# An attention-and-experts kernel on one core: attention re-ordered by unit with the k side ahead, the kv copy on ACT's own DMA queue, routing in pieces, and expert slots by rank with eight early slots

## The chip, the cores and the metric

One core of a Trainium2 chip. The metric is the device time of one execution in microseconds. Times are medians of executions; the span is the time from the first to the last instruction in one profiled execution, 1.6 to 1.9 us shorter than the time of that execution. (The profiled execution of the kernel before took 435.7 us, 4.5 below its median, so its stages are some 1% short.) All ratios compare executions of state "fast" only. Engines are named as the profile names them: PE (matmul), PEld (its weight loads), DVE, ACT, POOL, SP. Inputs are the same draw in every run.

## The reference, cut to what matters

```python
# q, k, v: 8 batches x 8 heads x 576 positions x 64
q_p, k_p = phi(q), phi(k)              # relu, times cos and sin of the position: 128 features
kv  = einsum('bhsf,bhsd->bhfd', k_p, v)
num = einsum('bhsf,bhfd->bhsd', q_p, kv)
den = einsum('bhsf,bhf->bhs', q_p, k_p.sum(2)) + 1e-6
x   = (num / den) as 4608 tokens of 512
e_idx = argmax(x @ w_gate)             # 8 experts, one per token
out   = gate * sigmoid(x @ w_output_gate)[e_idx] * (relu(x @ w1[e]) @ w2[e])
```

Attention is done in four groups of two batches. Its rows are scattered by expert into a buffer in DRAM (`xs`), and the experts then run 43 *slots* of 128 rows of one expert each. A table in SBUF says for each slot which expert it is and where its rows begin. Because the expert is known only at run time, the engines load table entries into registers.

## The kernel before

The slot loop. PE works through x transposes of the next slot, h transposes of the last one, first layer (`hp`, 8 matmuls), second layer of the last slot (`yp`, 8 matmuls). Two register loads stand between the transposes and the first layer.

```python
def layer1(j):
    ev = PE.value_load(evs[0:1, j:j + 1], min_val=0, max_val=7)      # which expert
    wv = PE.value_load(wns[0:1, j:j + 1], min_val=32, max_val=256)   # weights that must be in
    PE.wait_ge(wsem, wv)
    ...
    for fh in range(2):
        ...                                   # 4 matmuls on wt[:, ev, ...], then relu on ACT

for j in range(NSLOT + 1):
    if j + 4 < NSLOT: fetch(j + 4)            # SP: 128 rows of xs, at a row from the table
    if j + 1 < NSLOT: x_tr(j + 1)             # PE transposes, DVE copies xts
    if j >= 1:        hts = h_tr(j - 1)       # PE transposes, DVE copies hts
    if j < NSLOT:     layer1(j)
    if j >= 1:        layer2(j - 1, hts)      # PE, then DVE scales y, POOL scatters it
    ...
```

All routing is finished, and the table made in one block on DVE, before slot 0. In attention, heads are paired so that each query matmul finds its kv in its own half of the partitions; there is no copy of kv. v is loaded by 64 DMAs with rows of 256 B.

Of the kernel before, what the change touches and what calls it, by code (L numbers as in the profile page):

```python
# [21 lines left out]
def kernel(  # L22
# [12 lines left out]
    PE = nc.tensor  # L35
# [15 lines left out]
    NSLOT = 43  # L51
    XW = DM + 4
# [60 lines left out]
    for qd in range(4):  # L113
        hA = 4 * (qd // 2) + qd % 2
        for ab in range(2):
            h = hA + 2 * ab
            DVE.tensor_copy(wpr[0:64, qd, 32 * ab:32 * ab + 16], wg0[0:64, h, :])
            DVE.tensor_copy(wpr[64:128, qd, 32 * ab + 16:32 * ab + 32],
                            wg0[64:128, h, :])
# [16 lines left out]
    jv_i = constp.tile([P, NSLOT], I32, name="jv_i")  # L136
    GP.iota(jv_i[:], pattern=[[1, NSLOT]], base=0, channel_multiplier=0)
    jv = constp.tile([P, NSLOT], F32, name="jv")
# [8 lines left out]
                      iota8[:].unsqueeze(1).to_broadcast([P, E, E]), ALU.is_ge)  # L147

# [9 lines left out]

    EW = 4 * F + 8 * DM
# [3 lines left out]
    wsem = tc.alloc_semaphore("wsem")  # L163

    def load_w(e):
        for d in (GP.dma_start(w1v[:, e], moe_w1[e].rearrange("(c p) f -> p c f", p=128)),
                  GP.dma_start(w2v[:, e],
                               moe_w2[e].rearrange("(c p) d2 -> p c d2", p=128))):
            d.then_inc(wsem, 16)
            tc.add_to_no_dep_group("w", d.ins)  # L170

    def own(e, lo):
        return wt[:, e, lo:lo + 4096].bitcast(F32)

    kbuf = [own(7, 4096 * i).rearrange("p (h c d) -> p h c d", h=H, d=D) for i in range(2)]
    qbuf = [own(6, 4096 * i).rearrange("p (h c d) -> p h c d", h=H, d=D) for i in range(2)]
    KW = H * NC4 * 65 * 2
    v0 = wt[:, 4:6, :].rearrange("p e w -> p (e w)")
    vbuf = [v0[:, KW * i:KW * i + KW].bitcast(F32).rearrange(
        "p (h c d) -> p h c d", h=H, d=65) for i in range(2)]  # L180
    for i in range(2):
        GP.memset(vbuf[i][:, :, :, 64:65], 1.0)
# [3 lines left out]
    evs = constp.tile([P, NSLOT], I32, name="evs")  # L186
    wns = constp.tile([P, NSLOT], I32, name="wns")
    rows_i = constp.tile([P, NSLOT], I32, name="rows_i")
    valid = constp.tile([P, NSLOT], U8, name="valid")
    sidx = constp.tile([P, NSLOT], I32, name="sidx")  # L190
    GP.memset(sidx[:], BIG)

    with tc.tile_pool(name="wk", bufs=2) as wk, \
         tc.tile_pool(name="pqo", bufs=2, space=bass.MemoryType.PSUM) as pqo, \
         tc.tile_pool(name="pkv", bufs=1, space=bass.MemoryType.PSUM) as pkv, \
         tc.tile_pool(name="ptr", bufs=2, space=bass.MemoryType.PSUM) as ptr:



        zt = wk.tile([P, XW], U16, name="zt", tag="xr", bufs=14)  # L200
# [3 lines left out]
        tails, kvps, kvms, kcs, qrs, qTs, us = {}, {}, {}, {}, {}, {}, {}  # L204
        ktcs = {}

        def halves(dst, src, b, w=D):
            for hf in range(2):
                SP.dma_start(dst[:, 4 * hf:4 * hf + 4, :, 0:D],
# [6 lines left out]
        def load_v(b):  # L216
            for h in range(H):
                SP.dma_start(vbuf[b % 2][:, h, :, 0:D],  # L218
                             v[b, h, 0:512, :].rearrange("(p c) d -> p c d", c=NC4))
# [22 lines left out]
        def k_prep(b, c):  # L242

            if c == 4 and b % 2 == 1:
                return
            nm = "kc" if c < 4 else "ktc"
            kc = wk.tile([P, 2, H, D], F32, name=f"{nm}{b}_{c}", tag=nm,
                         bufs=2 if c < 4 else 1)
            src = kbuf[b % 2][:, :, c, :] if c < 4 else tails[b // 2, "k"][:]
            ACT.activation(kc[:, 0], src, AF.Relu, scale=cosc[:, c:c + 1])  # L250
            DVE.tensor_scalar(kc[:, 1], src, sinc[:, c:c + 1], 0.0, ALU.mult, ALU.max)  # L251
            if c < 4:
                kcs[b, c] = kc
            else:
                ktcs[b // 2] = kc

        def k_mm(b, c):
# [4 lines left out]
            kc = kcs.pop((b, c)) if c < 4 else ktcs[b // 2]  # L262
            p0, p1 = (0, P) if c < 4 else (lo, lo + 64)
            for hf in range(2):
                for pr in range(2):
                    for cs in range(2):
                        for ab in range(2):
                            h = 4 * hf + pr + 2 * ab
                            rhs = (vbuf[b % 2][:, h, c, :] if c < 4
                                   else vtl[p0:p1, h, :])  # L270
                            o = 130 * pr + 65 * cs
                            PE.matmul(kvp[64 * ab:64 * ab + 64, hf, o:o + 65],  # L272
                                      kc[p0:p1, cs, h, :], rhs,
                                      start=(c == 0 and pr == 0 and cs == 0),
                                      stop=(c == 4), skip_group_check=True)


        def g_evac(b):
            kvp = kvps[b]
            kvm = wk.tile([P, 8, 81], F32, name=f"kvm{b}", tag="kvm", bufs=3)  # L280
            kvms[b] = kvm
            DVE.tensor_copy(kvm[:, 0:4, 0:65],
                            kvp[:, 0, 0:260].rearrange("p (a w) -> p a w", w=65))
            ACT.copy(kvm[:, 4:8, 0:65],
                     kvp[:, 1, 0:260].rearrange("p (a w) -> p a w", w=65))
            kvc = wk.tile([P, 8, 64], F32, name=f"kvc{b}", tag="kvc", bufs=1)
            DVE.tensor_copy(kvc[:], kvm[:, :, 0:64])
# [181 lines left out]
        for i, (b, c) in enumerate(units):  # L469
            g = b // 2  # L470
            if c == 0:

                if b + 1 < B:
                    load_q(b + 1)
# [224 lines left out]
```

## Time and profile before

Median 440.2 us in the runs beside the changed kernel. Stages of the profiled execution (span 433.8 us), read from the PE timeline; the prediction shows the busy times:

| stage | us |
|---|---|
| start to first query matmul | 38.4 |
| group 0 / 1 / 2 / 3 of attention | 37.5 / 39.8 / 56.7 / 34.4 |
| last attention matmul to first expert matmul ("handover") | 37.3 |
| experts, first to last matmul | 182.0 |
| tail | 7.7 |

(The prediction puts the border between groups 2 and 3 at 170.8, inside the last unit of group 2; the first query matmul of group 3 starts at 172.4, and the tables here use that.)

One slot on PE's timeline (start, duration, engine, line, output and inputs, count; a bracket would give idle time before it):

```profile
301.00 1.89 PE L635 MATMUL yp<-wt,hts 128*128 x8
302.73 0.39 PE L595 MATMUL xtsp<-ident,xg 128*128 128x128 f16 x4
302.95 0.61 PE L607 MATMUL htsp<-ident,hs 128*128 128x128 f16 x8
303.40 1.89 PE L623 MATMUL hp<-wt,xts 128*128 x8
```

There is no bracket (gaps under 0.15 us get none): from `hp` at 299.28 to `hp` at 303.40 the array does not wait, 4.12 us per slot.

### The profile page before, as it was taken

The numbers are of one execution on the slowest core, as the hardware profiler recorded it, in microseconds if no ns is written. First come the engines' busy times: TensorE is split into PE (matmuls) and PEld (weight loads), VectorE is DVE, ScalarE is ACT, GpSimd is POOL, SyncE is SP. The second block draws the span as 40 slices with busy tenths as digits, with TensorE's granted clock in tenths as the row PEclk, the third lists the DMA queues.
The fourth block names the chain that finished last, engine by engine and source line by source line (L and its number), as shares of the span: only waits on it lengthen the run. The fifth ranks groups of instructions, "written<-read, shape, count | busy, mean of one in ns | idle before, by whom it ended". The sixth has DMA issues, their size and how long they took to land.

```text
span 433.8 us, 10053 instructions
## 1 busy us (share of the span) xinstructions
PE 319.4 (74%) x3468; PEld 214.5 (49%) x3468; DVE 205.7 (47%) x616; ACT 160.4 (37%) x291; POOL 142.8 (33%) x192
## 2 busy tenths in 40 slices
PE   0706897988885647974100499999999999999991
PEld 0605786766674536753000255555555555555550
DVE  6102576886767125775560234344443443434431
ACT  1304587675756235664100132322323323223230
POOL 2000232338635444248476024221222222212221
PEclk9965999999899577999555699999999999999998
DMA  7999694897899986804916999992323223233100
GB/s 160 243 206 300 175 225 134 223 249 225 196 218 203 327 206 133 131 16 88 202 61 131 225 217 188 222 239 88 110 74 103 94 78 111 63 101 110 62 25 0
DMA packets 90719, 66.88 MB, mean 154 GB/s; under 512 B 51886, under 2 KB 83118, under 8 KB 90672
## 3 DMA queue, kind: packets, MB, share of 16 engines
q1 hardware_dynamic: 72960, 35.26, 33.2%
q0 software_dynamic: 17712, 30.98, 31.4%
q8 instruction: 31, 0.51, 0.5%
q14 instruction: 16, 0.13, 0.1%
HBM read 67.61 MB, written 17.22 MB: 196 GB/s over the span
## 4 chain that ended last, share of the span: by engine, by line
issue 31%; DMA 18%; PE 17%; POOL 13%; DVE 8%; SPq 7%; ACT 3%; POOLq 1%; another core or an unknown queue 0%; DVEq 0%; ACTq 0%
DMA xs<-xr,di 12%; POOL out_dram L643 9%; PE qo L340 6%; PE kvp L272 6%; SPq L218 4%; DMA wt<-in_v_dram 4%; PE qtp L322 3%; POOL xs L428 3%; DVE u L352 2%; DMA wt<-in_q_dram 2%; DMA vtl<-in_v_dram 1%; ACT t L351 1%; SPq L447 1%; DVE kc L251 1%; PE kvtp L294 1%
## 5 line engine op out<-in xcount | busy, mean ns | idle before, releaser
L628 ACT ACTIVATE hs<-hp 128x512 f16<-128x512 f32 x86 | 51.3, 597 | 155.9 <-PE hp L623 155.9
L643 POOL DMA_INDIRECT out_dram<-ysb,sidx x43 | 42.6, 991 | 143.8 <-DVE ysb L641 140.8
L623 PE MATMUL hp<-wt,xts 128*128 x344 | 82.5, 383 | 2.4 <-DVE sidx L600 1.2
L635 PE MATMUL yp<-wt,hts 128*128 x344 | 81.3, 379 | 1.1 <-DVE hts L609 1.1
L360 POOL TENSOR_TENSOR xr<-u,rc 128x512 f16<-128x512 f32 x36 | 40.9, 1137 | 121.6 <-DVE rc L359 121.5
L641 DVE TENSOR_SCALAR ysb<-yp,xg 128x512 f32<-128x512 f32 x43 | 32.3, 750 | 102.4 <-PE yp L635 102.4
L272 PE MATMUL kvp<-wt,kc 128*64 128x65 f32 x1024 | 41.4, 240 | 22.5 <-ACT kc L250 13.8
L352 DVE SCALAR_TENSOR_TENSOR u<-qo,sinc,t 128x324 f32<-128x324 f32 x72 | 37.4, 552 | 40.8 <-ACT t L351 32.4
L340 PE MATMUL qo<-kvm,qT 64*128 64x162 f32 x512 | 48.3, 331 | 8.7 <-ACT qT L324 2.7
L635 PEld LDWEIGHTS <-hts 128*128 128x128 f16 x344 | 33.7, 98 | 41.5 <-DVE hts L609 1.2
L272 PEld LDWEIGHTS kvp<-wt,kc 128*64 128x64 f32 x1024 | 36.9, 152 | 27.9 <-issue 14.6
L623 PEld LDWEIGHTS <-xts 128*128 128x128 f16 x344 | 32.6, 99 | 34.2 <-issue 3.0
L351 ACT ACTIVATE t<-qo,cosc 128x324 f32<-128x324 f32 x72 | 36.9, 529 | 30.7 <-PE qo L340 25.1
L340 PEld LDWEIGHTS qo<-kvm,qT 64*128 64x128 f32 x512 | 40.3, 203 | 12.9 <-ACT qT L324 6.2
L428 POOL DMA_INDIRECT xs<-xr,di x36 | 35.8, 995 | 10.0 <-POOL xr L427 9.8
L595 PE MATMUL xtsp<-ident,xg 128*128 128x128 f16 x172 | 17.1, 223 | 27.6 <-DMA xg<-xs 27.6
L322 PE MATMUL qtp<-ident,qr 128*128 128x128 f32 x144 | 25.4, 303 | 13.1 <-ACT qr L315 13.1
L595 PEld LDWEIGHTS <-xg 128*128 128x128 f16 x172 | 13.3, 99 | 37.6 <-DMA xg<-xs 27.9
L609 DVE COPY hts<-htsp 128x1024 f16<-128x1024 f16 x43 | 29.2, 680 | 0.3 <-PE htsp L607 0.3
L598 DVE COPY xts<-xtsp 128x512 f16<-128x512 f16 x43 | 17.8, 414 | 20.7 <-PE xtsp L595 19.7
L607 PE MATMUL htsp<-ident,hs 128*128 128x128 f16 x344 | 26.4, 219 | 0.2 <-ACT hs L628 0.2
L322 PEld LDWEIGHTS qtp<-ident,qr 128*128 128x128 f32 x144 | 16.3, 149 | 20.0 <-ACT qr L315 14.9
(131 smaller groups left out, 293.7 us busy)
## 6 DMA issues: line engine op xcount, KB each, us to landing
wt<-in_moe_w_dram POOLq DMA_DIRECT2D x16, 1024.0 KB, 14.6
wt<-in_k_dram SPq DMA_DIRECT2D x16, 512.0 KB, 6.2
wt<-in_v_dram SPq DMA_DIRECT2D x64, 128.0 KB, 5.5
wt<-in_q_dram SPq DMA_DIRECT2D x16, 512.0 KB, 6.0
xg<-xs SPq DMA_DIRECT2D x43, 129.0 KB, 2.4
xs<-zt SPq DMA_DIRECT2D x9, 129.0 KB, 4.7
kt<-in_k_dram SPq DMA_DIRECT2D x8, 128.0 KB, 3.8
vtl<-in_v_dram SPq DMA_DIRECT2D x8, 128.0 KB, 4.6
```

The lines of the kernel that those rows point to most:

```text
L272: PE.matmul(kvp[64 * ab:64 * ab + 64, hf, o:o + 65], kc[p0:p1, cs, h, :], rhs, start=(c == 0 and pr == 0 and cs == 0), stop=(c == 4), skip ...
L322: PE.transpose(tp[:, i, :], qrf[:, 128 * i:128 * i + 128], ident[:])
L340: PE.matmul(qo[:, 2 * ab + pr, 0:162], lhs, kvms[b][r0:r0 + 64, 2 * qd:2 * qd + 2, :], start=True, stop=True)
L351: ACT.activation(t[:], qo[:, :, 0:81], AF.Copy, scale=cosc[:, c:c + 1])
L352: DVE.scalar_tensor_tensor(u[:, 4 * hf:4 * hf + 4, :], qo[:, :, 81:162], sinc[:, c:c + 1], t[:], ALU.mult, ALU.add)
L360: GP.tensor_tensor(xrow[:, 0:DM].bitcast(F16).rearrange("p (h d) -> p h d", d=D), u[:, :, 0:64], rc[:].unsqueeze(2).to_broadcast([P, H, D] ...
L428: d = GP.indirect_dma_start(out=xs[:, :], out_offset=bass.IndirectOffsetOnAxis(ap=di[:, c:c + 1], axis=0), in_=xr[:], in_offset=None)
L623: mm = PE.matmul(hp[:], xts[:, kc, :], wt[:, bass.ds(ev, 1), kc * F + fh * 512:kc * F + fh * 512 + 512], start=(kc == 0), stop=(kc == 3))
L628: ACT.activation(hs[:, fh * 512:(fh + 1) * 512], hp[:], AF.Relu)
L635: mm = PE.matmul(yp[:], hts[:, fc, :], wt[:, bass.ds(ev, 1), 4 * F + fc * DM:4 * F + fc * DM + DM], start=(fc == 0), stop=(fc == 7))
L641: DVE.tensor_scalar(ysb[:], yp[:], xg[:, DM + 2:DM + 4].bitcast(F32), None, ALU.mult)
L643: d = GP.indirect_dma_start(out=out[:, :], out_offset=bass.IndirectOffsetOnAxis(ap=sidx[:, j:j + 1], axis=0), in_=ysb[:], in_offset=None, ...
```

## The change

Its intent: start PE sooner (v in large rows, k side up to three units ahead), take routing out of long blocks, and fill the hole at the handover by letting the first eight slots run on tiles of experts that are already full after three groups, with weights loaded in order of that rank. A new query layout makes kv needed in both partition halves, hence a copy. The core of a long diff:

```diff
         def load_v(b):
-            for h in range(H):
-                SP.dma_start(vbuf[b % 2][:, h, :, 0:D],
-                             v[b, h, 0:512, :].rearrange("(p c) d -> p c d", c=NC4))
+            halves(vbuf[b % 2], v, b)                 # two DMAs, rows of 1 KB
 ...  # k_prep: a copy of v into rows of 65 on ACT
+                ACT.copy(vc[:, :, 0:D], vbuf[b % 2][:, :, c, :])
 ...  # the kv copy
+        def g_dup(b):
+            kvd = kvds[b]
+            ACT.dma_start(kvd[0:64, 8:16, :], kvd[64:128, 0:8, :])
+            ACT.dma_start(kvd[64:128, 8:16, :], kvd[0:64, 0:8, :])
 ...  # routing and tables are generators, one step() per unit or three per slot
+            if j == 0:
+                pending.append(late_table())          # slots 8 to 42
 ...  # slots
-            ev = PE.value_load(evs[0:1, j:j + 1], min_val=0, max_val=7)
-            wv = PE.value_load(wns[0:1, j:j + 1], min_val=32, max_val=256)
-            PE.wait_ge(wsem, wv)
+            PE.wait_ge(wsem[0], wa)      # wa, wb: loaded one slot ahead
+            PE.wait_ge(wsem[1], wb)
+        def regs(j):
+            evr[j] = [PE.value_load(tcol(m, j), min_val=lo, max_val=hi)
+                      for m, lo, hi in ((0, 0, 7), (1, 16, 112), (3, 16, 144))]
 ...  # the loop
+            if j >= 1 and j + 1 < NSLOT:
                 x_tr(j + 1)
             if j >= 1:
                 hts = h_tr(j - 1)
             if j < NSLOT:
                 layer1(j)
             if j >= 1:
                 layer2(j - 1, hts)
+            if j + 1 < NSLOT:
+                regs(j + 1)
+            for _ in range(3):
+                step()
```

Two semaphores now count the weights, so PE loads three numbers per slot (rank, two thresholds) and loads them one slot ahead, after the second layer.

## The prediction

> **What bounds the kernel now.** I read the page's second part (40 slices) first, for stages.
>
> ```profile
> PE   0706897988885647974100499999999999999991
> PEclk9965999999899577999555699999999999999998
> DMA  7999694897899986804916999992323223233100
> ```
>
> One slice is 10.8 us. From slice 23 on (experts) PE is full at full clock and DMA is at a third; before it PE is 60 to 90% busy, with a hole at slices 2-3, a dip at 12-14 while DMA is full, and four almost empty slices, 18 to 22. The timeline gives the borders: first query matmul at 38.4 us, groups of two batches (nine units each) start at 75.9, 115.7 and 170.8, the last attention matmul ends at 206.8, the first expert matmul starts at 244.1, the last ends at 426.1. Over these stretches I asked for the busy times (columns: stretch, us, then PE, PEld, DVE, ACT, POOL with counts, granted clock, DMA share, GB/s):
>
> ```profile
> 75.90:115.70 39.80, 32.63 (x566) 27.57 (x567) 30.20 (x90) 27.25 (x52) 22.92 (x29) 0.96 0.83 224
> 115.70:170.80 55.10, 36.85 (x558) 31.66 (x562) 26.54 (x86) 24.90 (x47) 23.00 (x30) 0.78 0.99 218
> 170.80:206.80 36.00, 25.41 (x398) 20.64 (x391) 26.49 (x82) 22.15 (x44) 19.83 (x26) 0.99 0.49 91
> 206.80:244.10 37.30, 1.79 (x21) 1.31 (x20) 13.27 (x55) 1.01 (x3) 19.08 (x28) 0.50 0.69 144
> 260.00:426.10 166.10, 165.01 (x1111) 89.31 (x1109) 71.07 (x156) 46.98 (x79) 42.38 (x44) 1.00 0.40 110
> ```
>
> Group 1 is bound by PE with little slack (32.6 of 39.8). Group 2 has the same work but takes 15 us more, at DMA 0.99. Handover: 37 us without PE. Experts: PE all the time. The waits and the chain say who ended the holes:
>
> ```profile
> PE xtsp L595 <- DMA xg<-xs: 27.6, 2, 26.7
> PE qtp L322 <- ACT qr L315: 13.1, 1, 13.1
> PE kvp L272 <- DMA wt<-in_v_dram: 8.7, 3, 4.9
> DVE u L352 <- POOL xr L360: 8.3, 4, 4.1
> 130.09 15.67 DMA wt<-in_v_dram
> ```
>
> The first is the handover: fetches wait for the slot table, made after the last routing, and for its scatters on POOL. The second is the start: the first q load lands at 35.15 us, behind 16 small v loads and nine zero stores. The third and fifth: in group 2 v loads land late, beside two weight loads. The fourth: at the end of group 3, POOL's scatters hold up the row products, these the u buffers.
>
> [...]
>
> ```profile
> DMA packets 90719, 66.88 MB, mean 154 GB/s; under 512 B 51886, under 2 KB 83118, under 8 KB 90672
> ```
>
> 64 v loads x 512 rows of 256 B are 32,768 of the 51,886, because v lands in rows of 65. While v goes with k (12 to 16 us) the trace moves 179-201 GB/s; at 34 to 36, mostly q and k, 361. [...] the trace has 0.50 at 206.8-244.1, and the first eight expert matmuls take 3.19 us against 1.89 later. So a hole costs another one to two microseconds after it.
>
> **The change part by part.**
>
> *Start.* v comes in two DMAs per batch instead of eight (1 KB rows), q before k of batch 1, and zero stores move to unit 5. SP pays about 0.63 us per issue, so 14 v issues fewer are 9 us and the nine stores 4.5 us. k, v, tails, q of batch 0 are 3.7 MB, some 15 us. ACT then sets the k side: per chunk a v copy into 65-wide rows (estimate 0.63, as qr's 0.626 for equal shape) and relu 0.725, from v's landing at about 12: five chunks end at 18, matmuls at 19.3. Then evacuation 1.3, kvtp 0.65, kvT 0.6, query transpose, kvgp 0.66, copy 0.3: 23.5; and new, the half-swap of kv by two ACT DMAs, 1.2 to issue and about 2.5 to land: 27.5. Against 38.4: -11.
>
> *A unit.* PE's work stays: qo 1.30, qtp 0.59, kvp 1.12 per chunk, kvtp 0.6, kvgp 0.6, routing 0.73. A group of nine with two batches of k side is 11.7 + 5.3 + 11.2 + 2.5 + 0.7 = 31.5. ACT loses the 36 relu passes of qr (22.5 us; relu goes into the transposes' evacuation) and gains 32 v copies (20 us): a group is qT 5.3, t 9.5, v 5.0, k 6.5, evacuations 1.9, exps 0.5, DMA issue 2.4 = 31. DVE: u 9.9, output for two chunks at a time 7.1 (was 10), k 4.9, kv 2.3, routing 5.2 = 29. So three engines stand at 29 to 31.5; none has much slack, and both qo buffers now belong to one unit, released by ACT and DVE only after all eight matmuls. Gained is the wait between evacuation and kvtp, now a unit apart (2.5 us per batch before, at 51.8 and 68.7), and the routing in threes instead of a block (85 to 94 in the chain). I take 36 for groups 1 and 2 (before 39.8 and 55.1): -4 and -19, the latter because both weight loads leave group 2, and v's packets shrink to a quarter. Demand then is 3.5 MB per batch, 18 us, 195 GB/s, under the 224 of group 1.
>
> *Groups 0 and 3.* "Three units ahead" moves k work forward: group 0 does 13 chunks and not 10, 35 us of PE, and batch 1's copy sits at the end of unit 3 with its first use in unit 4, 6 us of chain in the open. 43, against 37.5: +5.5. Group 3 keeps two chunks, 21 us of PE; the loop qo, t, u, next qo (1.3 + 0.06 + 0.55 + 0.6, or t, t, qT 1.7) and DVE at 3.3 per unit bound it: 30.5 against 36, -5.5.
>
> *Handover.* The first eight slots come from tiles already full after three groups. I worked out the router from the reference: counts then are 305, 416, 565, 0, 674, 568, 114, 814; the rank by two groups is expert 4, 2, 7, 1, 6, 5, 0, 3; full tiles 5 and 4, so slots 0-4 are expert 4 and 5-7 expert 2: the table always fills. What remains after the last matmul: DVE u, output, last early piece, about 4 us; but POOL has in the last three units four row products (1.14 each) and nine scatters (0.97 + gap; the copy at each is gone, so about 1.1): 14.5 us in 6.6, so the last scatter of group 2 issues 4.6 after the end; it lands 3.8 later (median of the issues), fetch 2.4 plus issue 0.6, transposes, copy and the second slot 1.6: 13. Against 37.3: -24.
>
> *Experts.* Same matmuls, 43 slots at 4.12 = 177, before 182. The remaining routing and late table, some 45 DVE operations of 0.2 to 0.5, fall into the first four slots: 6 to 7 us of DVE in slots 1 and 2 against 4.12, some 4 us slip; the weight wait at 249 (1.2) goes. 184: +2. Weights: rank 2 is issued at slot 4 and used from slot 13, 37 us for 14.6-23 us loads; the others have more. Tail 7.7, unchanged.
>
> Sum: 27.5 + 43 + 36 + 36 + 30.5 + 13 + 184 + 7.7 = 377.7 of span, against 433.8. Measured times lay 1.9 (profiled) to 6.4 us above it. I predict 379.
>
> **The rivals.** (a) ACT takes the bound: [...] has v copies and DMA issues (each waiting on DVE) between evacuations. For it: 31 against PE's 31.5. Then groups 0 to 2 take 41-46 each, about 395. Against it: before ran group 1 with DVE at 30.2 in 39.8 despite stalls. (b) The pipeline works as meant: PE over 95% in groups 1-2 (33), no stall at unit 4, group 3 at 27: about 364. For it: between 56.9 and 67 PE has gaps of 0.2 us only. (c) The early slots don't help: POOL's queue (weight load of rank 1 waits for rank 0[...]) shifts the wait to the fetch or to slot 5. Rank 1 is issued about 3 us after the attention and has some 30 until slot 5; if it came at 35 or POOL lagged 10 us more, 390. (d) DMA still bounds groups 0-2: if 220 GB/s were the cap whatever the packets, group 0's 12 MB would take 55, giving 390.
>
> **Range and chances.** All single failures leave it under 400, so faster is nearly sure: 0.98, within 2% 0.01, slower 0.01. (a) and (c) together give the high end, (b) the low: 363 to 396.
>
> **What would show it.** First qo at 25-30 us; groups 1-2 at 34-38 us each with PE above 85%, ACT above 80%, DMA below 0.85; no v wait over 2 us; PE idle 10-16 us at the handover, ended by a fetch behind a scatter on POOL; packets under 512 B down to about 19,000; expert stretch 181-187. It is wrong if groups 1-2 are over 40, if the hole moves to slot 5 or 8, or if expert slots rise above 4.2 us after the eighth.

## The result

The changed kernel took 457.5 us (median of four runs, 456.2 to 463.2, the longest slow) against 440.2 in the same rounds: ratio 1.038, 95% interval 1.032 to 1.044, so slower. Ratios here and below are the mean time of one kernel's fast runs over that of the other's fast runs of the same rounds, and so not quite the quotient of the medians quoted.

That was not the whole result. The same text was run twice more: 441.7 us, ratio 1.003 (0.996 to 1.010), and 458.8 us, ratio 1.036 (1.030 to 1.042). The kernel before stood at 440 to 442 each time. So about 62 us of the error against 379 are there every time, and 16 more come and go with the occasion.

| stage (us of span) | before | predicted | changed, 1st set | changed, 2nd set |
|---|---|---|---|---|
| start | 38.4 | 27.5 | 27.2 | 27.3 |
| group 0 | 37.5 | 43 | 57.0 | 57.0 |
| group 1 | 39.8 | 36 | 45.4 | 38.5 |
| group 2 | 56.7 | 36 | 42.4 | 35.3 |
| group 3 | 34.4 | 30.5 | 35.0 | 34.7 |
| handover | 37.3 | 13 | 16.5 | 18.3 |
| experts | 182.0 | 184 | 226.3 | 222.8 |
| tail | 7.7 | 7.7 | 6.9 | 6.9 |

The first expert matmul really does come 21 to 33 us sooner than before (223.4 and 211.1 against 244.1). The experts lose 41 to 44. The slices of the first set (tenths of busy time in 40 equal stretches of 11.4 us):

```profile
PE   0529749798789968681455897889888899899883
PEclk9965859899889987955597899999999999999998
```

From the 26th slice to the last but one PE is at 8 and 9 at full clock, where before it was a row of 9s. That is the slots. The stages of the first set (stretch, us, then PE, PEld, DVE, ACT and POOL busy with counts, granted clock, DMA share, GB/s):

```profile
27.20:84.20 57.00, 40.99 (x653) 35.05 (x653) 21.99 (x53) 28.82 (x55) 9.19 (x8) 0.73 0.74 216
84.20:129.50 45.30, 37.88 (x568) 30.57 (x566) 25.52 (x75) 25.76 (x52) 16.77 (x17) 0.89 0.68 199
129.50:171.90 42.40, 35.91 (x572) 29.03 (x567) 26.29 (x73) 24.97 (x50) 20.29 (x20) 0.94 0.52 154
206.90:223.40 16.50, 1.35 (x18) 1.27 (x19) 10.07 (x33) 1.31 (x4) 7.34 (x8) 0.50 0.73 147
260.00:449.70 189.70, 165.29 (x1076) 82.91 (x1076) 72.46 (x150) 38.88 (x38) 49.41 (x51) 1.00 0.61 136
```

PE is the fullest engine in these groups, but only 72, 84 and 85% of the time, so it is waits that lengthen attention; beside them the granted clock of group 0 was 0.73 (0.50 in two stretches, 26.9 to 43.9 and 54.2 to 67.8 us). In the last line PE is busy 165 of 190 us; the kernel before, from the same moment to the end of its experts, was busy 165 of 166 for about the same matmuls. The waits name who ended them (engine, output, line, what it waited for: us in total, times, longest):

```profile
PE xtsp L631 <- PE yps L682: 17.8, 33, 0.8
PE qo L378 <- DMA wt<-wt: 17.3, 5, 6.5
PE yps L682 <- DVE hts L649: 11.4, 3, 6.1
PE qo L383 <- issue: 7.0, 13, 1.0
```

Each of these four lines led to an experiment. The third is explained under "The late table"; the fourth is what comes and goes. All four are from the first set; the second set has the first three too (17.5, 18.1 and 7.2 us) and not the fourth.

*The slot.* PE's timeline late in the changed kernel:

```profile
406.14 1.89 PE L682 MATMUL yps<-wt,hts 128*128 x8
408.52 0.39 PE L631 MATMUL xtsp<-ident,xg 128*128 128x128 f16 x4 [0.49 <-PE yps L682]
408.75 0.61 PE L646 MATMUL htsp<-ident,hs 128*128 128x128 f16 x8
409.19 1.89 PE L667 MATMUL hp<-wt,xts 128*128 x8
```

`hp` to `hp` is now 4.78 us. "Waits for PE yps" sounds like a dependency between matmuls, but nothing in the transposes needs `yps`; the bracket only says that `yps` was what ended last before them. The sequencer's own records show what lies between: 

```profile
L653 PEldq TENSOR_LOAD <-tab x111: 295/302/948, 263.0 to 441.5; - x111
```

Three loads per slot, here at 406.48, 407.16 and 407.84, so 0.68 us apart: 0.30 for the load itself, 0.15 for a register operation, 0.02 for a bounds test, the rest between these records. The last is done at 408.46 and the transposes begin at 408.51.

*The first wait for the kv copy.*

```profile
27.23 0.88 PE L378 MATMUL qo<-wt,qT 64*128 64x162 f32 x2 [0.49 <-DVE wt L341]
34.37 2.52 PE L378 MATMUL qo<-wt,qT 64*128 64x162 f32 x14 [6.26 <-DMA wt<-wt]
```

The first matmuls come at 27.23, the predicted 27.5, but they are those that don't need the copy. The rest of the unit waits 6.26 us for it, and runs at a granted clock of 0.50 after, as it was in the wait (2.52 us for 14 instead of some 1.3).

### The profile page after: what moved, and what is told of

It reads as the page before. It is cut to its first block, busy times and chain, and to the rows that moved or that the text cites. A ratio compares the mean times of both kernels' runs of the same rounds, so it can differ in the third digit from the quotient of the medians.

```text
span 456.6 us, 10089 instructions
## 1 busy us (share of the span) xinstructions
PE 343.1 (75%) x3468; PEld 221.1 (48%) x3468; DVE 210.2 (46%) x589; ACT 146.3 (32%) x244; POOL 137.1 (30%) x161
## 2 busy tenths in 40 slices
DMA packets 66654, 69.52 MB, mean 152 GB/s; under 512 B 18606, under 2 KB 58030, under 8 KB 66608
## 3 DMA queue, kind: packets, MB, share of 16 engines
q1 hardware_dynamic: 47616, 35.25, 27.5%
## 4 chain that ended last, share of the span: by engine, by line
issue 30%; DMA 26%; PE 24%; POOL 10%; DVE 3%; ACT 2%; SPq 1%; POOLq 1%; ACTq 0%; DVEq 0%
DMA out_dram<-ysb,sidx 10%; PE kvp L303 9%; PE qo L378 8%; DMA wt<-wt 7%; POOL out_dram L693 6%; DMA out_dram<-ysb,xg 5%; POOL xs L482 3%; PE qtp L361 3%; DMA wt<-in_v_dram 2%; PE qo L383 2%; DMA xg<-xs 2%; PE kvgp L336 1%; PE kvtp L326 1%; POOL xr L403 1%; DVE wt L393 1%
## 5 line engine op out<-in xcount | busy, mean ns | idle before, releaser
L673 ACT ACTIVATE hs<-hp 128x1024 f16<-128x1024 f32 x43 | 44.0, 1023 | 178.2 <-PE hp L667 169.0
L682 PE MATMUL yps<-wt,hts 128*128 x344 | 84.4, 390 | 11.4 <-DVE hts L649 11.4
L689 DVE TENSOR_SCALAR ysb<-yps,xg 128x512 f32<-128x512 f32 x43 | 32.3, 751 | 122.0 <-PE yps L682 116.7
L403 POOL TENSOR_TENSOR xr<-wt,rc 128x512 f16<-128x512 f32 x36 | 40.9, 1152 | 131.8 <-DVE rc L401 131.7
L378 PE MATMUL qo<-wt,qT 64*128 64x162 f32 x512 | 57.0, 347 | 25.0 <-DMA wt<-wt 17.3
L378 PEld LDWEIGHTS qo<-wt,qT 64*128 64x128 f32 x512 | 46.3, 212 | 30.6 <-DMA wt<-wt 13.5
L682 PEld LDWEIGHTS <-hts 128*128 128x128 f16 x344 | 34.2, 99 | 53.9 <-DVE hts L649 12.3
L393 DVE SCALAR_TENSOR_TENSOR wt<-qo,sinc,wt 128x324 f32<-128x324 f32 x72 | 36.8, 550 | 45.0 <-ACT wt L390 42.3
L303 PE MATMUL kvp<-wt 128*64 128x65 f32 x1024 | 41.1, 244 | 17.7 <-ACT wt L288 16.8
L390 ACT ACTIVATE wt<-qo,cosc 128x324 f32<-128x324 f32 x72 | 34.6, 527 | 57.5 <-PE qo L378 46.0
L303 PEld LDWEIGHTS kvp<-wt 128*64 128x64 f32 x1024 | 37.4, 157 | 22.8 <-issue 22.5
L631 PE MATMUL xtsp<-ident,xg 128*128 128x128 f16 x172 | 18.1, 232 | 39.0 <-PE yps L682 17.8
```

The costliest lines, as they stand in the source:

```text
L303: PE.matmul(kvp[64 * ab:64 * ab + 64, s_ // 2, o:o + 65], kc[p0:p1, cs, 2 * s_ + ab, :], vc[p0:p1, 2 * s_ + ab, :], start=(c == 0 and s_ % ...
L378: PE.matmul(qos[a][:, m, 0:162], qT[r0:r0 + 64, m, :], kvds[b][r0:r0 + 64, 2 * sl:2 * sl + 2, :], start=True, stop=True)
L390: ACT.activation(t, qos[a][:, :, 0:81], AF.Copy, scale=cosc[:, c:c + 1])
L393: DVE.scalar_tensor_tensor(dst, qos[a][:, :, 81:162], sinc[:, c:c + 1], t, ALU.mult, ALU.add)
L403: GP.tensor_tensor(xrows[:, slot + x, 0:DM].bitcast(F16).rearrange("p (h d) -> p h d", d=D), u[:, 8 * x:8 * x + 8, 0:64], rc[:, 8 * x:8 * ...
L673: ACT.activation(hs[:], hp, AF.Relu)
```

## The experiments

Sixteen runs. Those up to the version with three mends were written down before the second set of the changed kernel was known, so their expectations start from 457; measured, they show no stall of the kind that made the first set slower, and 442 is the level to compare with. I therefore convert: gain = (1.003 - ratio) x 441 us, 1.003 being the ratio of the second set.

| run | median us | ratio to before | 95% | gain over changed kernel, us |
|---|---|---|---|---|
| loads spread | 430.0 | 0.973 | 0.969 to 0.977 | 13 |
| before, three loads | 465.2 | 1.052 | 1.048 to 1.057 | (23 lost against before) |
| copy on SP | 439.0 | 0.994 | 0.992 to 0.997 | 4 |
| no copy (wrong result) | 416.9 | 0.945 | 0.940 to 0.951 | 25 |
| one load | 412.8 | 0.939 | 0.932 to 0.946 | 28 |
| copy by PE | 431.9 | 0.977 | 0.974 to 0.981 | 11 |
| late table in pieces | 432.3 | 0.979 | 0.975 to 0.984 | 10 |
| three mends | 394.5 | 0.893 | 0.887 to 0.900 | 48 |
| changed kernel, 2nd set | 441.7 | 1.003 | 0.996 to 1.010 | 0 |
| changed kernel, 3rd set | 458.8 | 1.036 | 1.030 to 1.042 | (stalls) |
| weights after fetch | 391.8 | 0.890 | 0.881 to 0.899 | 50 |
| copy later | 389.2 | 0.884 | 0.878 to 0.890 | 52 |
| weights earlier | 407.8 | 0.921 | 0.916 to 0.925 | (stalls) |
| copy later, again | 391.2 | 0.891 | 0.886 to 0.896 | 49 |
| scatters earlier | 387.0 | 0.880 | 0.875 to 0.886 | 54 |
| tail loads later | 395.8 | 0.897 | 0.891 to 0.904 | 47 |

(The first set of the changed kernel is the result itself. The converted gains carry the intervals of both ratios, about 3 to 5 us either way. The rows from "weights after fetch" on are built on the version with three mends.)

### Register loads in the slot

Loads spread over the slot, one before the first layer, one between the layers, one after:

```diff
+            reg(j + 1, 0)
             if j < NSLOT:
                 layer1(j)
+            reg(j + 1, 1)
             if j >= 1:
                 layer2(j - 1, hts)
-            if j + 1 < NSLOT:
-                regs(j + 1)
+            reg(j + 1, 2)
```

> The changed kernel with the three register loads that PE makes per expert slot no longer in a row after the second layer's matmuls, but one before the first layer, one between the layers, one after the second layer. Theory A (the lengthened slot is PE's sequencer, held 2.05 us by three loads in a row while its lead over the array is about 1.6 us): slots after the eighth fall from 4.78 to 4.12-4.2 us and the whole time falls by 22 to 29 us, to 429-436. Rival (the slot is longer because relu now runs once per 1024 columns, or because first-layer and transpose buffers are shared with the attention's pools): slots stay at 4.7-4.8 and the time stays within 3 us of 457.

The total fell into the expected range, and for the wrong reason: half of it was the missing stalls. The slots fell to a median of 4.52 us, not to 4.12. So the place of the loads is part of it and not all.

The reverse, on the kernel before, its loads moved behind the second layer and a third, unused one added:

```diff
-            ev = PE.value_load(evs[0:1, j:j + 1], ...)
-            wv = PE.value_load(wns[0:1, j:j + 1], ...)
             ...
                 layer2(j - 1, hts)
+            if j + 1 < NSLOT:
+                regs(j + 1)        # the same two loads, and wns once more
```

> The reverse on the kernel before: its two register loads per slot are moved to after the second layer's matmuls and a third, unused one is added, all else unchanged. Theory A: its slots grow from 4.12 to about 4.75 us, and the time from 440 to 464-470. Rival (single relu of 1024 columns or shared buffers, which the kernel before does not have): no change, 439-442.

Slots of 4.79 us in the median instead of 4.12, time +23 us, in a kernel that has neither the single relu nor the shared buffers. The rival is out: the loads alone make the loss.

One load per slot in the changed kernel, the two thresholds worked out in registers:

```diff
-            evr[j] = [PE.value_load(tcol(m, j), ...) for m, lo, hi in (...)]
+            evr[j] = [PE.value_load(tcol(0, j), min_val=0, max_val=7)]
 ...
-            PE.wait_ge(wsem[0], wa)
-            PE.wait_ge(wsem[1], wb)
+            PE.wait_ge(wsem[0], (ev >> 1) * 32 + 16)
+            PE.wait_ge(wsem[1], ((ev + 1) >> 1) * 32 + 16)
```

> The changed kernel with one register load per slot instead of three, at the same place after the second layer; PE works the two wait thresholds out of the expert's rank with register operations. After the spread loads brought slots to 4.5 and not to 4.12, two readings are left. Reading A1 (the place: a burst of loads outlasts the sequencer's lead): one load of 0.68 us fits in the lead of 1.6, slots fall to 4.12-4.2. Reading A2 (the rate: the sequencer needs 16 x 0.134 = 2.1 us for the addresses of the weights and 3 x 0.68 = 2.05 for the loads plus some 0.3 of waits, 4.5 in all, whatever the order): with one load it needs about 3.2 plus the new register operations, under the array's 4.12, so slots of 4.12 too, but it also explains 4.5 in the spread version, which A1 does not. Both give 427-432 in all if the attention is as in the changed kernel, less 8 if the stalls in the tail units stay away as they did with spread loads. Slots still at 4.4 or more would refute both.

Median slot 4.12 us, gain 28 us. PE's timeline:

```profile
385.01 1.89 PE L666 MATMUL hp<-wt,xts 128*128 x8
386.73 1.89 PE L681 MATMUL yps<-wt,hts 128*128 x8
388.46 0.22 PE L631 MATMUL xtsp<-ident,xg 128*128 128x128 f16 x1
```

The three versions fit one account, an estimate from the sequencer's records. Per slot the sequencer needs 16 register operations for the weights' addresses, 0.134 us apart (2.1 us), and 0.68 per load. With three loads that is 2.1 + 2.05 + about 0.3 for waits = 4.5, more than the array's 4.12, however they are placed: the spread version's 4.52. In one burst, there is in addition nothing dispatched far enough ahead to cover it: the lead at that place was about 1.6 us (loads begin at 406.48, the array runs out at about 408.03) against 2.05: 4.78. With two loads (2.1 + 1.4 + 0.3 = 3.8), as before, or one, the array is the bound.

### The kv copy

The copy on SP's queue, ahead of the loads that used to be issued before it:

```diff
-            ACT.dma_start(kvd[0:64, 8:16, :], kvd[64:128, 0:8, :])
-            ACT.dma_start(kvd[64:128, 8:16, :], kvd[0:64, 0:8, :])
+            SP.dma_start(kvd[0:64, 8:16, :], kvd[64:128, 0:8, :])
+            SP.dma_start(kvd[64:128, 8:16, :], kvd[0:64, 0:8, :])
 ...
-        load_q(1); load_k(2); load_v(2)
         k_do(0, "evac")
 ...
         k_do(0, "dup")
+        load_q(1); load_k(2); load_v(2)
```

> The changed kernel with the kv copy issued on SP's queue in program order ahead of the loads of q, k and v that used to be issued just before it, in place of ACT's own queue. Theory B (the copy lands late [...] 4 us to the first packet against 1 us when SP was idle): the five waits of PE's first query matmuls for the copy fall from 17.3 us to under 7, group 0 shrinks by 6 to 10 us, and the whole time falls by 6 to 12 us, to 445-451. Rival (the copy is slow because the 16 engines are full of load data, whichever queue it is on): waits stay near 17 us and the time within 3 us of 457, or rises because loads now queue behind a copy that waits for DVE.

PE's waits for the copy added up to 16.5 us, so the expectation failed in the sum, though group 0 fell to 50.2 us as expected. Copy by copy it is clear. From the DMA packets in the traces (a copy is 128 packets of 2,592 B), with the count of 512 KB and tail loads that SP issued in the 8 us before:

```
                      issue    SP loads before   first packet   landed
changed, 2nd set      27.20          5              +4.3          +6.3
  (ACT's queue)       56.21          6              +4.5          +6.5
                      80.86          4              +1.6          +6.5
                      98.26          6              +4.2          +7.2
                     117.06          2              +1.1          +2.8
                     133.59          6              +4.0          +6.7
                     151.80          2              +1.2          +4.3
                     169.42          0              +1.1          +2.7
copy on SP            26.50          1              +1.2          +2.8
  (SP's queue)        51.74          0              +1.1          +2.7
                      77.62          6              +3.7          +8.3
                      97.29          5              +4.0          +7.8
                     116.56          2              +1.1          +2.9
                     133.09          5              +3.1          +6.5
                     151.03          2              +1.2          +4.5
                     168.76          0              +1.2          +2.7
```

("Landed" is the end of the last packet. The semaphore that PE waits for follows 0.5 to 1.1 us later in the five copies for which the trace pairs it: 3.2 us after the issue with nothing queued, 7.1 to 8.7 in the slow ones.)

What decides is whether several loads were issued just before (80.86, with four, lies between: it begins soon and ends late); which queue the copy is on makes no difference at like loads (98.26 and 97.29, 117.06 and 116.56). The DMA engines' share from the issue to the first packet was full in both kinds of case (1.08 at 98.26, 1.04 at 117.06), so full engines alone are not it either: it is the loads already issued. In the version on SP the first two copies were ahead of the loads and landed in 2.8 and 2.7 us, where ACT's took 6.3 and 6.5; the third stood behind tail loads and landed in 8.3, and PE waited 9.3 us for it. ACT's first issue of a copy took 0.47 to 0.56 us in the first set, 0.47 both in a slow case (97.58) and with nothing queued (182.64), so the wait is not in the issuing. In the trace some 900 to 1,700 packets of SP's loads went first in the slow cases. The first fetch of the slots waits as long (2.6 to 4.2 us, below) behind weights that POOL issued on another queue. What holds the first packet back is not shown: no run here separates the ways of queueing.

No copy at all, a wrong result, as a bound:

```diff
-            elif w == "dup":
-                g_dup(b)
+            elif w == "dup":
+                pass
 ...
-                        sl = h // 2 + (0 if h % 2 == a else 4)
+                        sl = h // 2
```

> Wrong result on purpose: the changed kernel without the kv copy, the query matmuls reading the half that is already there, so that nothing waits for it. It bounds what the copy costs. If the copy's landing is all that separates group 0 from its prediction of 43 us, group 0 falls from 57 to 43-46 us, and the whole time by 14 to 18 us, to 439-443; if the stalls named issue in the tail units and the loads set the groups, the time falls by less than 8 us because the waits move to the next thing.

Group 0 is 40.1 us, groups 1 and 2 31.9 and 33.6: better than predicted. All of attention, first to last query matmul, is 138.7 us against 165.5 in the second set. The gain of 25 us in time (not the 40 of the medians) bounds what the copy costs in all: its waits, the clock of 0.50 after them, the two DMA issues on ACT and its traffic, which this run does not separate. (Its tokens, and so its routing, are wrong; its experts took 220.6 us against 222.8.)

The copy by PE instead, with a swap matrix:

```diff
-            ACT.dma_start(kvd[0:64, 8:16, :], kvd[64:128, 0:8, :])
-            ACT.dma_start(kvd[64:128, 8:16, :], kvd[0:64, 0:8, :])
+            for x in range(2):
+                sp = ptr.tile([P, 512], F32, ...)
+                for y in range(2):
+                    PE.matmul(sp[:, 162 * y:162 * y + 162], swp[:],
+                              kvd[:, 4 * x + 2 * y:4 * x + 2 * y + 2, :], start=True, stop=True)
+                ...                       # x = 0: DVE copies 324 columns back, x = 1: ACT
```

> The changed kernel with the kv half-swap made by PE (four matmuls of 162 columns with a swap matrix per batch, about 0.65 us) and two evacuations of 324 columns, one on DVE and one on ACT, instead of two DMAs. If the copy's latency is what costs the 40 us that the version without a copy gained, this keeps most of it: attention from first qo to its end 142-152 us against 179.6, the groups near 42, 34, 35, 31, and the whole time 420-430. If the version without a copy gained because its ACT, DMA engines and SBUF had less to do, the gain here is smaller than 20 us.

```profile
27.59 1.34 PE L352 MATMUL kvsp<-wt,swp 128*128 128x162 f32 x8 [0.48 <-DVE wt L344]
28.86 1.47 PE L390 MATMUL qo<-wt,qT 64*128 64x162 f32 x16
```

The first full unit starts 1.3 us after the swap, and the copies never show as waits for a DMA. But only 11 us are gained, not 25: the swap made PE stand for DVE's copy of `kvgp` in front of it (0.48 us here), and units that were short before are longer: units 1 of groups 1 to 3 took 6.5, 11.3 and 7.9 us against 4.6, 5.1 and 5.4 without a copy. The waits of 0.5 us are too short for all of that; the rest is not taken apart. Attention is 154.7 us, 10.8 less than in the second set; it and the time of 431.9 lie just outside the ranges expected. A gain under 20 us was what the other reading foretold, that the version without a copy also gained from less work for ACT, the DMA engines and SBUF, so that reading is not out.

Swapping after the unit's own query matmuls was tried on top of other mends:

```diff
-            if steps[i] and steps[i][0][1] == "dup":
-                k_do(*steps[i].pop(0))          # at the very start of the unit
             for f in todo: ...
```

> The version before this one, with the swap matmuls of the kv copy issued after the unit's own query matmuls and not at its very start, where PE stands waiting for DVE's copy of kvgp. Units 1 of groups 1 to 3 took 6.5, 11.3 and 7.9 us with the swap against 4.6, 5.1 and 5.4 without any copy, units 3 and 7 some 2 us more: expected are 2 us per group back in groups 1 to 3, so about 5 to 8 us less, 383-386. If it is DVE's and POOL's stretched operations that make those units long, it stays at 390.

389.2 us, and 391.2 when repeated, against 391.8 for the version it was built on: nothing that the intervals would show. (Of the stretched operations that the expectation names, DVE's can be seen: in the version with three mends a product of 128 columns took 2.65 us at 106.45, one of 256 columns 0.42 us at 103.89; what stretched it was not shown. POOL's row products were not longer in the mean, 1.14 us with the copy by PE against 1.15 in the first set of the changed kernel.) In group 1 the time left units 1 and 6 and came back in units 2 and 7 (5.1 and 4.8 us instead of 3.0).

### The late table

PE's two long waits in the first slots of the changed kernel, first set:

```profile
241.43 3.57 PE L682 MATMUL yps<-wt,hts 128*128 x8 [6.13 <-DVE hts L649]
251.84 3.32 PE L682 MATMUL yps<-wt,hts 128*128 x8 [4.23 <-DVE hts L649]
```

and in the second set:

```profile
226.18 1.89 PE L682 MATMUL yps<-wt,hts 128*128 x8 [3.26 <-DVE hts L649]
234.90 3.34 PE L682 MATMUL yps<-wt,hts 128*128 x8 [2.87 <-DVE hts L649]
```

The second layer waits for `hts`, a copy of 0.69 us. DVE's timeline of the first set shows why: 15 table operations from 235.48 to 239.88, then xts, then hts at 240.59; and 22 more from 245.71 on. Three pieces per slot were thought small, but one of them has ten operations and the last has eighteen, and they stand in DVE's order ahead of the two copies that PE needs next. After both holes of the first set and the second hole of the second set eight matmuls take 3.3 to 3.6 us, where they otherwise take 1.89; in the first set the granted clock was 0.50 and 0.55 there, and 1.00 in the later slots. The second set shows what the table costs by itself; in the first set a stall (last section of the experiments) adds to the first hole. The mend puts nine smaller pieces (the expectation says ten) between hts and the scaling of y, where DVE has nothing else to do:

```diff
                 hts = h_tr(j - 1)
+            for _ in range(3):
+                step()
             if j < NSLOT:
                 layer1(j)
             ...
-            for _ in range(3):
-                step()
 # and a yield more in the first piece, two more in the last
```

> The changed kernel with the late table in ten pieces of about 1 us, three per slot and put between the copy of hts and the scaling of y on DVE, where DVE waits about 3.5 us for PE anyway, in place of six pieces, three per slot, after the scaling. Theory C (slots 2 and 3 took 12.3 and 10.2 us because 15 and 22 table operations stood on DVE ahead of xts and hts, with half clock after the hole): slots 1 to 4 take 4.8-5.5 each and the time falls by 10 to 14 us, to 444-448. Rival (those slots wait for weights or fetches): no change.

```profile
220.28 1.89 PE L670 MATMUL hp<-wt,xts 128*128 x8
222.00 1.89 PE L685 MATMUL yps<-wt,hts 128*128 x8
224.40 0.39 PE L634 MATMUL xtsp<-ident,xg 128*128 128x128 f16 x4 [0.51 <-PE yps L685]
225.08 1.89 PE L670 MATMUL hp<-wt,xts 128*128 x8
```

The holes are gone; the first five slots take 24.4 us, against 32.9 in the second set of the changed kernel and 37.5 in the first. Gain 10 us. What remains at 224.40 is the loads.

### The three mends together

> All three mends together: one load, copy by PE, late table in pieces. If the three causes are separate and add up (28 for the loads, 33 for the copy, 12 for the table), the time is 457 - 73 = 384, range 378-392: near what was predicted for the change, and 13% below the kernel before. If they overlap, the time stays above 395.

394.5 us, 48 below the changed kernel; the three gains one by one are 28 + 11 + 10 = 49. Within the intervals the three gains add up. (The 384 expected had counted the stalls into the gains.) The 42 slot intervals sum to 177.1 us, which with the last slot is the experts' 184 of the prediction.

### The handover

Weights of rank 1 after the first fetch:

```diff
-        wload = {30: 0, 35: 1}
+        wload = {30: 0}
 ...
         for j in range(EARLY):
             fetch(j)
+        load_w(1)
```

> The version with three mends, and the weights of rank 1 issued by POOL after SP's first fetch instead of 1 to 2 us before it. Theory D (the first fetch lands 6.5 us after its issue because it stands behind the 2 MB of weights issued just before, as the kv copy stood behind the loads; where nothing was queued ahead, a copy landed in 2.7 us): the fetch lands within 3 us, the first expert matmul comes 3 to 4 us earlier, and the time falls to about 391. Rival (the fetch is slow because the scatters of group 2 are still being written, or for its own packets): no change, and the weights of rank 1 come 3 us later at slot 5, which may cost 1 us.

The edit did not do what it was for: program order on POOL is not order between POOL and SP, and POOL still issued the weights at 188.67, before the fetch at 189.66. The first packet came 4.2 us after the fetch's issue, as before. So 391.8 us tells nothing on the theory. The weights of ranks 0 and 1 one and two units earlier, with the later copy kept:

```diff
-        wload = {30: 0, 35: 1}
+        wload = {29: 0, 33: 1}
```

> The version with three mends and the later copy, and with the weights of ranks 0 and 1 issued one and two units earlier, so that those of rank 1 are over when the slots' first fetch is issued (in the version meant to put them after the fetch, POOL still issued them 1 us before it, so it told nothing). Theory D (the first fetch stands behind the weights issued just before it, 3.6 to 4.1 us to its first packet): the first packet comes within 1.5 us, the first expert matmul 2 to 3 us sooner after the last of attention than the 17.8 us of before this, and the time falls by 2 to 5 us, to 384-387. Rival (scatters or its own packets make the fetch slow): first packet still at 3.5 us or more, time at 389. If the weights now lengthen group 3 instead, what is won at the fetch is lost there.

Now the first packet came 1.0 us after the issue and the 128 rows were in after 1.7, against 2.6 to 4.2 and 4.8 to 6.3 in the nine profiles of the changed kernel and its variants that I compared, where the weights went just ahead (in the kernel before, 3.7 and 5.8). These are the first 128 packets; the last step of the fetch's semaphore, for which PE waits, came 2.0 us after the issue, against 5.3 to 8.1 in the other profiles. The scatters are not the rival that they seem: in the version with scatters sooner, below, the last one was issued 7.6 us before the fetch, and its first packet still took 3.7 us, with weights issued 0.9 us ahead. Theory D holds for the fetch. The time doesn't show it: this was an occasion with stalls, SP had waited 11.9 us for a scatter of group 2, and the handover was 20.1 us. Whether earlier weights pay in the whole stays open.

Two routing pieces joined to their neighbours, so that group 2's scatters are over sooner:

```diff
             DVE.tensor_reduce(df[:], ds_[:], AX.X, ALU.add)
-            yield
 ...
             DVE.tensor_reduce(den[:, 0, :], ex[:], AX.X, ALU.add)
-            yield
```

> The control with two of the routing's pieces joined to their neighbours, so that POOL's nine scatters per group come two units earlier and not beside the tail unit of the next group. In the profiles with the stalls, the stalls of groups 1 and 2 lie beside six scatters. Theory E (scatters beside the tail unit's 64-row matmuls make the stall): where the control shows the stalls, this one does not and is 13 to 16 us faster; where the control has none, no difference but for some us at the handover, where the last scatter of group 2 comes sooner. Rival: the stalls stay in the tail units.

387.0 us, the fastest, 12% below the kernel before. The handover is 15.2 us and not 18.0 as in its control. Its stages, to be read against those of the changed kernel:

```profile
29.60:73.00 43.40, 39.27 (x669) 34.02 (x668) 23.61 (x58) 30.49 (x59) 9.55 (x9) 0.91 0.94 251
73.00:107.70 34.70, 33.51 (x586) 28.98 (x583) 24.83 (x70) 25.58 (x52) 17.40 (x18) 1.00 0.78 236
107.70:145.40 37.70, 33.84 (x585) 29.19 (x583) 29.17 (x77) 25.58 (x52) 20.64 (x21) 1.00 0.54 162
224.00:378.20 154.20, 151.76 (x1025) 81.49 (x1022) 65.78 (x144) 37.14 (x37) 45.70 (x47) 1.00 0.71 162
```

In group 1 PE is busy 33.5 of 34.7 us at full clock: this is what "bound by PE" looks like, and what the prediction had assumed. The control, for completeness:

> The fastest version so far (one load, swap on PE after the unit's own matmuls, late table in pieces; 389.2 us) once more, as a control for the next two and to see it on another occasion. Where the stalls in tail units appear it should be at 402-408, where they don't at 387-392.

### The stalls that come and go

> The changed kernel unaltered, on the chip of the other experiments. Its first profile had stalls of PE named issue in the tail units of groups 1 and 2 (10.8 and 11.3 us instead of 3.0 to 3.6), which none of the eight variants shows, though five of them have the same attention. If the stalls belong to that chip or that moment, this run has tail units under 4 us and a time of 438-444; if they belong to this program, they are back, and the time is 455-460.

> The changed kernel unaltered once more. Its first set of runs gave 457.5 us with two stalls of PE of 7.7 us each, named issue, in the tail units of groups 1 and 2; its second gave 441.7 on another occasion without them. If the stalls are a rare state of a chip or a moment, this set is at 440-443 again with tail units under 4 us; if they come back now and then, some of the six runs are near 457 or the profile shows them.

Second set: no stalls, 441.7. Third set: stalls, 458.8. They lie in the tail units (the ninth unit of a group, on the last 64 positions of two batches) of groups 1 and 2: 10.8 and 11.3 us in the first set, 3.0 and 3.6 in the second, 10.7 and 11.3 in the third. First set, group 1:

```profile
118.79 0.85 PE L383 MATMUL qo<-wt,qT 64*64 64x162 f32 x12
120.14 0.47 PE L383 MATMUL qo<-wt,qT 64*64 64x162 f32 x2 [0.50 <-issue]
121.58 0.43 PE L383 MATMUL qo<-wt,qT 64*64 64x162 f32 x2 [0.96 <-issue]
...
125.89 0.96 PE L383 MATMUL qo<-wt,qT 64*64 64x162 f32 x9 [0.73 <-issue]
```

and the same unit in the second set:

```profile
119.76 1.43 PE L383 MATMUL qo<-wt,qT 64*64 64x162 f32 x32
```

"issue" means that the engine waited for nothing that the profile shows. ACT and DVE, which wait there for matmuls that by the profile ended at 118.9, begin only at 125.95 and 126.01. The profile's end of a matmul is modelled (its page says so), so the trace leaves open whether PE or its signal was late. It was not ACT or DVE: PE's own semaphore updates for these matmuls are recorded at 125.93 and 125.99, 7.1 us after the computed end. That is how such a stall can be told in a trace. In the tail units of the three profiles with stalls the updates come 4.9 to 7.2 us after the computed end; in the other fifteen profiles no update of PE comes more than 2 us after it. Slots 2 and 3 are also longer with the stalls (12.3 and 10.2 us, 12.7 and 10.4 in the third set, against 9.1 and 8.8). The version with earlier weights, run on the same occasion as the third set, has them too: tail units of 8.7 and 9.4 us, and one slot of 12.9 us in which DVE begins 6.9 us after the matmuls it waits for have ended by the profile. The kernel before, run beside them all, shows nothing of it in its time. Two suspects were tried, POOL's scatters (above) and the small loads for the next tails:

```diff
-            if n == 3 * (b0 == 0) and g + 1 < NG:
+            if n == 3 and b0 == 0:
                 load_tails(g + 1)
+            if n == 2 and b0 > 0:
+                load_qtail(g)
+                if g + 1 < NG:
+                    load_tails(g + 1)
-            if n == 7 and g + 1 < NG:
-                load_qtail(g + 1)
```

> The control with the tail loads of the next group (rows of 256 B for q, k and v tails) issued in unit 2 of a group and no longer as soon as the tail unit's transposes and the last tail matmuls free their buffers, which is when the stalls begin. Theory F (these loads make the stall): where the control shows the stalls, they are gone here and 13 to 16 us with them; where it has none, a difference within 3 us. Rival: the stalls stay.

On that occasion the control had no stalls (391.2 us), so neither run could answer. The mean of the fast runs is 3 us above the control's, at the edge of the noise, and 2 us of it lie in the start of its profile, which the edit doesn't touch. The results name the chip: no stalls in the thirteen runs of the changed kernel and its variants on chips 11 and 12, and stalls in both runs on chip 2 (the first set is without a name). That is too few to call it the chip. The cause is open.

## Why the prediction was wrong, point by point

Right: the start (27.2, predicted 27.5); groups 1 and 2 where there are no stalls (38.5 and 35.3, predicted 36 each), tail, packets under 512 B (18,606, predicted about 19,000), v copies on ACT (0.62 us, estimated 0.63), no long waits for v after the start, ACT not the bound (24 to 29 us busy in groups 0 to 2). The rivals (a), (b) and (d) did not come. The direction of the handover was right. But ACT was busy 66 and 69% of groups 1 and 2 in the second set, not over 80% (25 us a group, and not the 31 of the working), and the sign "groups 1-2 over 40" came in the first and third sets, with the stalls. What the larger packets of v are worth by themselves is not shown by a run.

Wrong, in order of size, against the second set, whose 440.8 us of span are 63 over the predicted 377.7:

- *"Experts. Same matmuls, 43 slots at 4.12 = 177" and "some 4 us slip".* 39 us of the 63. The diff's third register load and its new place were in front of me; I counted matmuls and not what PE's sequencer has to do between them. The slot took 4.8 us, some 28 us in all, shown by the version with one load and by the reverse on the kernel before. The slip of the late table was sized by DVE's total work, not by its order before xts and hts, and without the slower matmuls after (3.3 to 3.6 us for eight): some 10 us instead of 4. So the term that failed is "43 slots at 4.12": PE's sequencer, not the array, set the slot. The prediction named its own test, slots above 4.2 us after the eighth, and that is what came.
- *"about 2.5 to land"* for the kv copy. In group 0, 14 us of the 63. The 2.5 was my estimate; the kernel before has no such copy (its fetches landed in 2.4 us in the median). It is near where nothing is queued (2.7 to the last packet, 3.2 to the semaphore), but six of eight copies were issued soon after four or more loads or beside others and took 4.3 to 7.2. What it leaves out is the longer wait for the first packet, 4.0 to 4.5 us in four of these six against 1.1 with nothing queued; from the first to the last packet the eight copies took 1.6 to 4.9 us.
- *"fetch 2.4 plus issue 0.6".* 5 us: the handover took 18.3, predicted 13. 2.4 was the median over all slots, taken beside little traffic; the first fetch stands behind 2 MB of weights, and PE's first transpose came 8.1 us after its issue, where 3.0 was predicted. In the version with earlier weights it was 2.0. (The working beside it has a slip: 14.5 us of POOL's work in 6.6 leaves 7.9 and not 4.6, which three units of 3.3 would give. The last scatter was issued 5.3 us after the end of attention, so this did not cost much.)
- Group 3, 34.7 against 30.5, 4 us: not taken apart by a run. As the kernel before took 34.4 from its first query matmul, the change gained nothing there; the predicted gain of 5.5 rested in part on the border at 170.8. DVE was its fullest engine, busy 28.3 of 34.8 us.

Beyond that, 16 us of the result are the stalls, which no reading of the kernel before could have shown, and which are unexplained. So the changed kernel is not a wrong idea: with one load, the copy off the DMA queues and the table placed behind hts it is 11% faster than the kernel before (on occasions without stalls), 12% with the scatters sooner. At 385.1 us of span that last version comes within 8 us of the predicted sum.

## What to carry to other kernels

Count what each engine's sequencer does per loop as carefully as what its array does: three register loads of 0.68 us and sixteen address computations made a loop of 4.12 us into one of 4.8, and the profile called it a wait for the last matmul. A DMA on another queue is not a DMA past the traffic (here 6.3 us with five loads ahead, 2.7 with none): put short, urgent transfers ahead of the loads in issue order, or keep them off DMA. Work moved out of a block into the gaps of a loop belongs behind the operations that the bounding engine waits for, in pieces no longer than the gap. And run a surprising result again on another occasion before explaining all of it.
